# Row-block buffers in the dense stage of a fused layer's training step, attention weights loaded among its row blocks, and the first left rows and masks kept on chip

## The chip, the cores and the metric

The kernel runs on one core of one Trainium2 chip, as a single launch. The metric is the device time of that launch in microseconds (us); less is better. Before the change, three runs took 2913.0, 2915.46 and 2922.69 us, so the median is 2915.46 us.

## What is computed

The reference is one layer, forward and backward. `xn` is the layer norm of `x` (2048 rows of 512). Two branches start from it, and the output is `x + attention(xn) + dense(xn)`; then come the gradients of ten inputs.

```
def _A_ref(x, mem0, Wq, Wk, Wv, Wo, seg_len):      # 64 segments of 32 rows, 8 memory rows, 32 heads of 128
    mem = mem0
    for s in range(n_seg):
        h = concatenate([mem, x of segment s])
        q, k, v = h Wq, h Wk, h Wv
        p = softmax(where(mask, q k^T * scale, -1e9))
        o = (p v) Wo
        mem = o[:, :M, :]                           # the next segment starts from these rows
        outs.append(o[:, M:, :])
def _B_ref(x, w1, b1, w2, b2):                      # 512 -> 1792 -> 512
    r = relu(x w1 + b1)
    return (r * r) w2 + b2
```

All arrays are bfloat16. The attention branch is a recurrence over 64 segments; the dense branch is not.

## The kernel before, in words

The launch has five stages, one behind the other: the dense branch with its backward pass (this is the stage that changes), the "left rows" (attention projections that can be made ahead of the recurrence), the forward recurrence, the backward recurrence with left blocks, and the weight gradients. The order inside the recurrences is written out by hand (`F_ORDER`, `B_ORDER`, under `manual_schedule`). In the dense stage and the left rows a scheduler places the instructions of each engine, the DMA issues of the SP queue among them; the order in the source is only its starting point.

**Dense stage (L176 to L329).** 2048 rows are worked in `NRB` = 4 row blocks of `RB` = 512 rows. Block `rb` does the following.

- `norm(rb)` (L193 to L218) normalises the rows on DVE (`bn_stats` L198, `xn` L206) with one `sqrt` on ACT (L202), stores them (`S_XN`, L209), turns them with 16 PE transposes (`ps_tr`) into `HT` (L215) and stores `HT` in four pieces (`S_HX`, L218). It is called for block `rb + 1` inside block `rb`, behind the second matrix product below.
- `ps_h` (L271): 14 groups of 4 matmuls; ACT makes `rT` = relu (L273), DVE makes `aT` = rT * rT (L274).
- `ps_ga` (L278): 14 groups of 4 matmuls on the turned output gradient `gT`; DVE makes `gh1T` (L280).
- Then, for each of four row chunks `rc` of 128 rows: `ps_B` (L302, 14 matmuls), evacuated by two DVE additions (L305, L307; the second adds `x`, read again from DRAM as `xb`, L297) and stored (`S_B`, L308); `ps_gxb` (L311, 14 matmuls), copied (L314) and stored (`S_GXNB`, L315); 28 transposes of `aT` and `gh1T` (`ps_trf`), copied into `Nt` (L323) and stored (`S_AN` and `S_GH1N`, L324). `Nt` has two buffers, so a chunk's copy waits until the store of the chunk before it has landed. All PSUM tiles of the stage turn through eight buffers (`pst`).

`HT` and `gT` hold all 2048 rows for the whole stage; `rT` and `gh1T` are two tiles. In the last block GpSimd copies the first 8 rows of each segment out of them into `xl` and `gl`, and those go to DRAM (`S_XL`, L259, and `S_GLT`, L264).

**Weights.** `weight_load(1)` fetches `Wk` (4 MB) in one DMA on SP (L182, placed by the scheduler into block 0). `Wq` and `Wv` (4 MB each) are fetched in the last block, after `ps_ga`, on GpSimd's queue, into the room that the tiles of pool `p1c` leave.

**Left rows (L334 to L366).** `XL0`, `XL1` (from `S_XL`) and `Wo` (4 MB) are loaded on SP (L356 to L358). 30 groups of 4 matmuls (`ps_L`, L349) follow in the order of `ALL_LEFT`: 8 groups with `Wk` and `XL0`, 6 with `Wk` and `XL1`, 8 with `Wq`, 8 with `Wv`. ACT and DVE copy each group into half of a `dNL` tile (L364; six buffers), and each full tile is stored into `S_NL` (L353, 15 stores).

**Start of the forward recurrence.** GpSimd builds the masks `maskA` and `maskl1` (L676 to L689), DVE copies `maskl1` into `maskL` (L697). `memN0` is loaded and turned by four small transposes (`ps_m0`), `X0` is loaded from `S_HX` (L961), and its memory rows are written by DVE (L962). The first projections (L391) read `X0`; their results go into `f_N` (L373, L376), whose room was that of some `dNL` tiles, and are then turned (`ps_tr`, L164).

Of the kernel before, what the change touches and what calls it, by code (L numbers as in the profile page):

```python
# [26 lines left out]
def kernel(  # L27
# [92 lines left out]
    S_XL = dram.tile([P, DC, S // SEG * M], BF16, name="S_XL")  # L120
# [33 lines left out]
    rstd_t = const.tile([P, TC], F32, name="rstd_t")  # L154

# [11 lines left out]
    ht_cm = sb("ht", 1)  # L167
    htp = ht_cm.__enter__()
    HT = htp.tile([P, DC, S], BF16, name="HT")

# [5 lines left out]

    RCB = RB // P
    wk_cm = sb("wk", 1, "right")
    Wqkv = [None, wk_cm.__enter__().tile([P, DC, HD], BF16, name="Wk"), None]

    def weight_load(t, q=dma):
        q(Wqkv[t][:], (A_Wq, A_Wk, A_Wv)[t].rearrange("(c p) h e -> p c (h e)", p=P))  # L182
    with sb("p1b", 2) as p1b, sb("p1", 1) as p1:
        p1c_cm = sb("p1c", 1)
        p1c = p1c_cm.__enter__()
        xq = {}

        def x_load(rb):
            xq[rb] = p1b.tile([P, RCB, D], BF16, name="xq", tag="xq")
            dma(xq[rb][:], xflat[rb * RB:(rb + 1) * RB, :].rearrange("(c p) d -> p c d", p=P))  # L190

        def norm(rb):

            x = xq[rb]
            bs_ = p1b.tile([P, RCB, 6], F32, name="bs_", tag="bs_")
            mv = p1b.tile([P, RCB, 2], F32, name="mv", tag="mv")
            for c in range(RCB):
                nc.vector.bn_stats(bs_[:, c, :], x[:, c, :])  # L198
                nc.vector.bn_aggr(mv[:, c, :], bs_[:, c, :])
            veps = p1b.tile([P, RCB], F32, name="veps", tag="veps")  # L200
            nc.vector.tensor_scalar(out=veps[:], in0=mv[:, :, 1], scalar1=EPS, scalar2=None, op0=ALU.add)
            nc.scalar.sqrt(veps[:], veps[:])  # L202
            nc.vector.reciprocal(rstd_t[:, rb * RCB:(rb + 1) * RCB], veps[:])
            xn = p1b.tile([P, RCB, D], BF16, name="xn", tag="xn")
            for c in range(RCB):
                nc.vector.tensor_scalar(out=xn[:, c, :], in0=x[:, c, :], scalar1=mv[:, c, 0:1],  # L206
                                        scalar2=rstd_t[:, rb * RCB + c:rb * RCB + c + 1], op0=ALU.subtract,
                                        op1=ALU.mult)
            dma(S_XN[rb * RB:(rb + 1) * RB, :].rearrange("(c p) d -> p c d", p=P), xn[:])  # L209
            for d0 in range(0, DC, 2):  # L210
# [4 lines left out]
                nc.any.tensor_copy(HT[:, d0:d0 + 2, rb * RB:(rb + 1) * RB], ps[:])  # L215
            for c in range(RCB):
                b0 = rb * RB + c * P
                dma(S_HX[b0 // P], HT[:, :, b0:b0 + P])  # L218

# [5 lines left out]
        gT = p1c.tile([P, DC, S], BF16, name="gT")  # L225

        def g_load(rb):
            nc.sync.dma_start_transpose(gT[:, :, rb * RB:(rb + 1) * RB], gflat[rb * RB:(rb + 1) * RB, :])
            dma(S_GT[:, :, rb * RB:(rb + 1) * RB], gT[:, :, rb * RB:(rb + 1) * RB])
# [11 lines left out]
        for f0 in range(0, FC, 2):  # L241
            nc.sync.dma_start_transpose(W1T[:, f0:f0 + 2, :], B_w1[:, f0 * P:(f0 + 2) * P])
        b2bc = p1.tile([P, D], BF16, name="b2bc")
# [6 lines left out]
        for rb in range(NRB):  # L250
            r0 = rb * RB
            if rb == NRB - 1:
                xl = p1c.tile([P, DC, NB * NL], BF16, name="xl", tag="xl")
                for dc in range(DC):
                    for q in range(NB // SPB):
                        nc.gpsimd.tensor_copy(
                            xl[:, dc, q * P:(q + 1) * P].rearrange("p (j t b) -> p b j t", t=M, b=SPB),
                            HT[:, dc].rearrange("p (q b j r) -> p q b j r", b=SPB, j=SPB, r=SEG)[:, q, :, :, 0:M])
                dma(S_XL[:], xl[:])  # L259
                gl = p1c.tile([P, DC, NB * NL], BF16, name="gl", tag="xl")  # L260
                for dc in range(DC):
                    nc.gpsimd.tensor_copy(gl[:, dc].rearrange("p (s t) -> p s t", t=M),
                                          gT[:, dc].rearrange("p (s r) -> p s r", r=SEG)[:, :, 0:M])
                dma(S_GLT[:], gl[:])  # L264
            rT = p1c.tile([P, FC, RB], BF16, name="rT")
            aT = p1.tile([P, FC, RB], BF16, name="aT")
            gh1T = p1.tile([P, FC, RB], BF16, name="gh1T")
            for fc in range(FC):
                ps = pst([P, RB], F32, name="ps_h1")
                for dc in range(DC):  # L270
                    nc.tensor.matmul(ps[:], lhsT=W1[:, dc, fc * P:(fc + 1) * P], rhs=HT[:, dc, r0:r0 + RB],  # L271
                                     start=(dc == 0), stop=(dc == DC - 1))
                nc.scalar.activation(rT[:, fc, :], ps[:], ACT.Relu, bias=b1T[:, fc:fc + 1], scale=1.0)  # L273
                nc.vector.tensor_tensor(out=aT[:, fc, :], in0=rT[:, fc, :], in1=rT[:, fc, :], op=ALU.mult)  # L274
            for fc in range(FC):
                ps2 = pst([P, RB], F32, name="ps_ga")
                for dc in range(DC):
                    nc.tensor.matmul(ps2[:], lhsT=W2T[:, dc, fc * P:(fc + 1) * P], rhs=gT[:, dc, r0:r0 + RB],  # L278
                                     start=(dc == 0), stop=(dc == DC - 1))
# [4 lines left out]
            if rb == NRB - 2:  # L284
                weight_load(1)
# [3 lines left out]
            else:  # L289
# [3 lines left out]
                for t, n in ((0, "Wq"), (2, "Wv")):  # L293
                    Wqkv[t] = wqp.tile([P, DC, HD], BF16, name=n)
                    weight_load(t, pdma)
            xb = p1b.tile([P, RCB, D], BF16, name="xb", tag="xb", bufs=1)
            dma(xb[:], xflat[r0:r0 + RB, :].rearrange("(c p) d -> p c d", p=P))  # L297
            for rc in range(RCB):
# [17 lines left out]
                for srcT, dstD in ((aT, S_AN), (gh1T, S_GH1N)):  # L316
# [7 lines left out]
                    dma(dstD[:, :, rr0 // P, :].rearrange("n p f -> p n f"), Nt[:].rearrange("p (n f) -> p n f", f=2 * P))  # L324
        gb1s = p1.tile([P, FC], F32, name="gb1s")
# [4 lines left out]
    ht_cm.__exit__(None, None, None)  # L330

# [8 lines left out]
    ALL_LEFT = (ALL_LEFT[:n_k] + ALL_LEFT[3 * n_k:3 * n_k + PER] + ALL_LEFT[n_k:3 * n_k] + ALL_LEFT[3 * n_k + PER:])  # L340
# [13 lines left out]
    with sb("fl", 2) as fl:  # L354
        XL0 = fl.tile([P, DC, P], BF16, name="XL0", bufs=1)
        dma(XL0[:], S_XL[:, :, 0:P])  # L356
        dma(XL1[:], S_XL[:, :, P:])
# [313 lines left out]
    with sb("fw", 1) as fw, psum("fr", 4) as fr, psum("fpp", 1) as fpp, \  # L671
            ExitStack() as fstack:

        KM = 4
        maskA = fw.tile([P, KM, KW], BF16, name="maskA")
        nc.gpsimd.memset(maskA[:], 0.0)  # L676
        maskL = fw.tile([P, KM, KW], BF16, name="maskL")
        maskl1 = fw.tile([P, 2, SPB, M], F32, name="maskl1")
        nc.gpsimd.memset(maskl1[:], 0.0)

        def keep(ap, pattern, base, mul):
            nc.gpsimd.affine_select(ap, ap, pattern=pattern, compare_op=ALU.is_ge, fill=-1e9, base=base,
                                    channel_multiplier=mul)

        for g in range(HG):
            sl = slice(32 * g, 32 * g + 32)

            keep(maskA[sl, :, M:SEG], [[0, KM], [-1, XS]], -M, 1)
            nc.gpsimd.memset(maskA[32 * g:32 * g + M, :, :], 0.0)  # L689

            keep(maskl1[sl, 0], [[-M, SPB], [0, M]], 0, 1)
            keep(maskl1[sl, 0], [[M, SPB], [0, M]], M - 1, -1)
            keep(maskl1[sl, 1], [[-M, SPB], [-1, M]], 0, 1)
            keep(maskl1[sl, 1], [[-M, SPB], [0, M]], 0, 1)
            keep(maskl1[sl, 1], [[M, SPB], [0, M]], M - 1, -1)
        for k in range(KM):
            nc.vector.tensor_copy(maskL[:, k, :], maskl1[:].rearrange("p a j m -> p (a j m)"))  # L697
# [11 lines left out]
        memN = fo.tile([M, D], BF16, name="memN0")  # L709
        dma(memN[:], mem0flat)  # L710
        psm0 = tr("ps_m0")
        for dc in range(DC):
            transpose_to(psm0[:, dc * M:(dc + 1) * M], memN[:, dc * P:(dc + 1) * P])
# [5 lines left out]
        def block(b):  # L719

            if b not in blk:
# [8 lines left out]
                def make(n):  # L730
                    pool, shape, dt = shapes[n]
                    return pool.tile(shape, dt, name=n, tag=n)
# [227 lines left out]
        X0 = block(0)["X"]  # L960
        dma(X0[:], S_HX[0])  # L961
        nc.vector.tensor_copy(X0[:, :, 0:M], psm0[:, 0:DC * M].rearrange("p (c m) -> p c m", c=DC))  # L962
# [19 lines left out]
    xl_cm.__exit__(None, None, None)  # L982
    assert not TURNS_O
# [3 lines left out]
    with sb("la", 2) as la, sb("ls", 2) as ls, sb("lo", 1) as lo_, sb("wg", 2) as wg, psum("lpp", 1) as lpp, psum("lr", 4) as lr:  # L987
# [122 lines left out]
        def keep(b, i, ps):  # L1110
# [4 lines left out]
            if "b2" in ps and i == 0:  # L1115
                ps["b2s"] = wg.tile([1, D], BF16, name="gb2b", bufs=1)
# [557 lines left out]
```

## Time and profile before

| | |
|---|---|
| median of the runs | 2915.46 us |
| time of the profiled execution | 2925.15 us |
| its span | 2923.3 us |
| mean granted TensorE clock | 0.973 |
| PE busy | 2721.1 us (93%) |
| DVE, ACT, POOL busy | 1297.6, 1030.6, 655.3 us |
| dense stage on PE | 9.71 to 262.4 us |
| left rows on PE | 268.18 to 296.4 us |
| first projection of the forward recurrence | 300.99 us |

The profile is one execution. The span runs from its first to its last instruction; 1.85 us of the execution's time lie outside it. A row of the timeline of an engine gives the start, the length, the line, the operation and tiles, the count, and in brackets the idle time ahead of it with what ended that. "Granted clock" is the share of TensorE's full clock in a stretch. On the SP queue the rows are DMA issues, not transfers; where an issue row is long, the queue was held.

### The profile page before, as it was taken

The page shows a single profiled execution, that of the slowest core. Times are in us where ns is not written, and L with a number is a line of the kernel's source. Part 1 is how long each engine was busy: PE and PEld are TensorE (multiplying, and loading weights), DVE is VectorE, ACT ScalarE, POOL GpSimd, SP SyncE. Part 2 cuts the span into 40 slices and gives each one's busy share as a digit, 9 for nine tenths or more (in the row PEclk, how much of TensorE's full clock was granted, in tenths as well). Part 3 has the DMA queues.
Part 4 walks back from the last instruction along what each step waited for, and adds up shares of the span by engine and source line. Part 5 has one row for each costly group of instructions (what it writes and reads, how often), then busy time and mean ns, then how long its engine had stood idle before and what let it go on. Part 6 is the DMA issues. An engine that isn't in the chain of part 4 may idle for free.

```text
span 2923.3 us, 116288 instructions
## 1 busy us (share of the span) xinstructions
PE 2721.1 (93%) x51700; PEld 1476.2 (50%) x51700; DVE 1297.6 (44%) x3790; ACT 1030.6 (35%) x2362; POOL 655.3 (22%) x1262
## 2 busy tenths in 40 slices
PE   7997899999999888889899999998999899999999
PEld 3453455555555555547445545554555444444444
DVE  5452466666666565444445544554455401100000
ACT  2332354444544444433333433433343301111111
POOL 0000100000000001122434343343333324332221
PEclk9998899999999999899899999999999999999999
DMA  9639367677776676999577777777777799999993
GB/s 249 214 101 292 94 166 191 178 193 184 181 196 171 166 170 167 230 260 259 145 181 176 175 197 202 177 183 201 189 172 184 215 280 226 222 211 234 205 206 79
DMA packets 796536, 564.17 MB, mean 193 GB/s; under 512 B 584593, under 2 KB 687138, under 8 KB 792706
## 3 DMA queue, kind: packets, MB, share of 16 engines
q1 hardware_dynamic: 753922, 424.58, 63.3%
q0 software_dynamic: 42112, 132.16, 14.4%
q8 instruction: 405, 6.64, 1.0%
q14 instruction: 97, 0.79, 0.1%
HBM read 191.51 MB, written 234.37 MB: 146 GB/s over the span
## 4 chain that ended last, share of the span: by engine, by line
PE 77%; DMA 11%; DVE 5%; SPq 3%; issue 3%; ACT 1%; POOL 0%; ACTq 0%; DVEq 0%; POOLq 0%
PE ps_gw L1635 17%; PE ps_proj L391 15%; PE ps_gR L459 11%; PE ps_R L459 5%; PE ps_L L349 3%; PE b_pp L589 3%; PE ps_tr L164 3%; PE ps_RL L1247 3%; DMA b_kLs<-S_NL 3%; PE ps_w L1102 2%; PE ps_sc L436 2%; PE f_pp L589 2%; PE b_T L494 1%; PE f_T L494 1%; PE ps_w L1097 1%
## 5 line engine op out<-in xcount | busy, mean ns | idle before, releaser
L1635 PE MATMUL ps_gw<-gn,HNc 128*128 128x512 bf16 x1920 | 416.8, 379 | 0.0
L1635 PEld LDWEIGHTS <-HNc 128*128 128x128 bf16 x1920 | 187.8, 98 | 223.6
L373 ACT CAST f_N<-ps_proj 128x512 bf16<-128x512 f32 x320 | 183.8, 580 | 202.5 <-PE ps_proj L391 200.9
L1568 ACT CAST wt<-ps_gw 128x512 bf16<-128x512 f32 x128 | 74.1, 587 | 450.6 <-PE ps_gw L1635 402.2
L391 PEld LDWEIGHTS <-X 128*32 128x32 bf16 x6144 | 154.3, 96 | 149.8 <-DVE X L503 21.4
L1551 DVE TENSOR_TENSOR gx<-ps_rows,gb 128x512 f32<-128x512 f32 x16 | 11.1, 692 | 426.6 <-PE ps_rows L1549 426.6
L891 POOL COPY kM<-f_kT 128x256 bf16<-128x256 bf16 x64 | 25.6, 400 | 739.9 <-DVE f_kT L376 565.9
L1635 PE MATMUL ps_gw<-GOc,gn 128*128 128x512 bf16 x640 | 141.6, 384 | 10.9 <-ACT wt L1568 9.4
L459 PE MATMUL ps_gR<-Wv,gv 128*32 128x512 bf16 x2048 | 145.9, 407 | 1.2 <-issue 1.2
L391 PE MATMUL ps_proj<-Wq,X 128*32 128x512 bf16 x2048 | 136.1, 382 | 7.2 <-DVE X L962 4.5
L459 PE MATMUL ps_gR<-Wk,gk 128*32 128x512 bf16 (+1 forms) x2048 | 141.1, 390 | 1.4 <-ACT gk L373 0.7
L373 ACT CAST gk<-b_pp 128x256 bf16<-128x256 f32 x192 | 70.7, 379 | 179.7 <-PE b_pp L589 116.0
L459 PE MATMUL ps_R<-Wo,OT 128*32 128x256 bf16 x4096 | 132.9, 286 | 1.1 <-DVE OT L376 1.1
L391 PE MATMUL ps_proj<-Wk,X 128*32 128x512 bf16 x2048 | 133.1, 384 | 0.7
L373 ACT CAST gON<-ps_proj 128x512 bf16<-128x512 f32 x128 | 74.9, 585 | 156.9 <-PE ps_proj L391 156.9
L391 PE MATMUL ps_proj<-Wv,X 128*32 128x512 bf16 x2048 | 129.9, 378 | 0.0
L391 PE MATMUL ps_proj<-Wo,GT 128*32 128x512 bf16 x2048 | 124.2, 384 | 4.2 <-DVE GT L1292 3.5
L1569 POOL DMA_DIRECT2D out_dram<-wt x120 | 64.8, 542 | 258.3 <-ACT wt L1568 243.5
L459 PE MATMUL ps_gR<-Wq,gq 128*32 128x512 bf16 (+1 forms) x2048 | 118.5, 343 | 0.9 <-issue 0.9
L1328 POOL COPY PD<-b_P 32x320 bf16<-32x320 bf16 x256 | 114.7, 448 | 8.0
L459 PEld LDWEIGHTS <-OT 128*32 128x32 bf16 x4096 | 108.1, 101 | 9.3 <-DVE OT L376 1.3
L1323 POOL DMA_DIRECT2D b_P<-S_A x63 | 33.8, 537 | 336.9 <-issue 103.5
(281 smaller groups left out, 5352.6 us busy)
## 6 DMA issues: line engine op xcount, KB each, us to landing
S_A<-f_N SPq DMA_DIRECT2D x64, 512.0 KB
out_dram<-wt POOLq DMA_DIRECT2D x134, 128.0 KB, 5.1
S_A<-f_N SPq DMA_DIRECT2D x64, 256.0 KB
S_GB<-gv SPq DMA_DIRECT2D x32, 512.0 KB
S_GB<-gq SPq DMA_DIRECT2D x32, 512.0 KB
S_GB<-gk SPq DMA_DIRECT2D x32, 512.0 KB
b_kN<-S_A POOLq DMA_DIRECT2D x63, 256.0 KB, 4.5
b_qN<-S_A POOLq DMA_DIRECT2D x63, 256.0 KB, 3.9
```

The source lines that it names most:

```text
L164: nc.tensor.transpose(ps_ap, in_ap, ident[base:base + k, base:base + k])
L349: nc.tensor.matmul(ps[:], lhsT=x(dc), rhs=Wqkv[t][:, dc, c0:c0 + 512], start=(dc == 0), stop=(dc == DC - 1))
L373: nc.scalar.copy(out, in_)
L391: nc.tensor.matmul(o, lhsT=hT[:, dc, :], rhs=x, start=(dc == 0), stop=(dc == DC - 1), tile_position=(0, 32 * g))
L436: nc.tensor.matmul(sc3[32 * g:32 * g + 32, k, c:c + n], lhsT=qT[:, 4 * h + k, g, :], rhs=kT[:, 4 * h + k, g, :], start=(mask is None), sto ...
L459: nc.tensor.matmul(R[32 * g:32 * g + 32, 0:(cs.stop - cs.start) * P].rearrange("p (a b) -> p a b", b=P), lhsT=XT(k, g), rhs=x[:, cs, :], s ...
L589: nc.tensor.matmul(o, lhsT=N_[32 * g:32 * g + m, kk * P:(kk + 1) * P], rhs=X(kk)[32 * g:32 * g + m], start=(i == 0), stop=(i == len(jobs) ...
L1247: nc.tensor.matmul(ps["R", i][32 * g:32 * g + 32, :].rearrange("p (a b) -> p a b", b=P), lhsT=B_[n][:, k, g, :], rhs=W(g * KH + k), start= ...
L1328: nc.gpsimd.tensor_copy(PD[32 * g:32 * g + 32, g], C["P"][32 * g:32 * g + 32, :, 0:L])
L1568: nc.scalar.copy(wt[:], ps[:])
L1569: eng(dst, wt[:])
L1635: nc.tensor.matmul(ps[:], lhsT=l(rc), rhs=r(rc), start=(n == 0), stop=(n == RC_ALL - 1))
```

## The change

- `HT` and `gT` become tiles of one row block (512 rows, one buffer each). `rT` and `gh1T` become one tile: relu is written into it, and the gradient replaces it in place.
- `x` has three buffers instead of two, and the addition of `x` (L307, now L345) reads it there; `xb` and its four loads go.
- `first_rows(rb)` copies each block's first rows on GpSimd as soon as the block is there. Those of the first 16 segments stay on chip (`XLa`); the rest go to DRAM once. The whole first 128 rows stay too (`Xa`), with the memory rows written into them in block 1 (`memN0`, four transposes, one DVE copy).
- `Wv` gets room of its own beside `Wk` from the start. The weights are fetched in 1 MB pieces on SP: one piece behind each row chunk, `Wk` in block 1, `Wv` in block 2, `Wq` in block 3, as the source has it. Nothing is fetched on GpSimd's queue in this stage.
- In the last block GpSimd copies `XLa` and `Xa` to `XL0` and `X0` and finishes the masks there; `maskA` is 40 columns wide instead of 64.
- The left rows go `Wk`/`XL0` (8 groups), `Wv`/`XL0` (8), `Wk`/`XL1` (6), `Wq`/`XL0` (8).
- `gb2b`, a small tile of a later stage, takes a turn in the buffers of `wt2`.

```diff
-    HT = htp.tile([P, DC, S], BF16, name="HT")
...
-    Wqkv = [None, wk_cm.__enter__().tile([P, DC, HD], BF16, name="Wk"), None]
-    def weight_load(t, q=dma):
-        q(Wqkv[t][:], (A_Wq, A_Wk, A_Wv)[t].rearrange("(c p) h e -> p c (h e)", p=P))
+    Wqkv = [None, wkp.tile([P, DC, HD], BF16, name="Wk"), wkp.tile([P, DC, HD], BF16, name="Wv")]
+    def weight_load(t, dc):
+        dma(Wqkv[t][:, dc], (A_Wq, A_Wk, A_Wv)[t].rearrange("(c p) h e -> c p (h e)", p=P)[dc])
...
-            xq[rb] = p1b.tile([P, RCB, D], BF16, name="xq", tag="xq")
+            xq[rb] = p1b.tile([P, RCB, D], BF16, name="xq", tag="xq", bufs=3)
...
+            HT = HTs[rb] = p1.tile([P, DC, RB], BF16, name="HT")
...
+        def first_rows(rb):
+            for dc in range(DC):
+                nc.gpsimd.tensor_copy(
+                    (xl[:, dc, (rb - 1) * P:rb * P] if rb else first["XLa"][:, dc]).rearrange("p (j t b) -> p b j t", t=M, b=SPB),
+                    HTs[rb][:, dc].rearrange("p (b j r) -> p b j r", b=SPB, j=SPB)[:, :, :, 0:M])
+                nc.gpsimd.tensor_copy(gl[:, dc, rb * P:(rb + 1) * P].rearrange("p (s t) -> p s t", t=M),
+                                      gTs[rb][:, dc].rearrange("p (s r) -> p s r", r=SEG)[:, :, 0:M])
+            if rb == 0:
+                nc.gpsimd.tensor_copy(first["Xa"][:, :, M:], HTs[0][:, :, M:P])
+            if rb == 1:
+                ps = pst([P, DC * M], BF16, name="ps_m0")
...
-            rT = p1c.tile([P, FC, RB], BF16, name="rT")
-            gh1T = p1.tile([P, FC, RB], BF16, name="gh1T")
+            rT = gh1T = p1.tile([P, FC, RB], BF16, name="gh1T")
...
-            if rb == NRB - 2:
-                weight_load(1)
...
-                for t, n in ((0, "Wq"), (2, "Wv")):
-                    Wqkv[t] = wqp.tile([P, DC, HD], BF16, name=n)
-                    weight_load(t, pdma)
-            xb = p1b.tile([P, RCB, D], BF16, name="xb", tag="xb", bufs=1)
-            dma(xb[:], xflat[r0:r0 + RB, :].rearrange("(c p) d -> p c d", p=P))
+                Wqkv[0] = wqp.tile([P, DC, HD], BF16, name="Wq")
+                XL0, X0 = (smp.tile([P, DC, P], BF16, name=n) for n in ("XL0", "X0"))
+                nc.gpsimd.tensor_copy(XL0[:], first["XLa"][:])
+                nc.gpsimd.tensor_copy(X0[:], first["Xa"][:])
+                maskA, maskL = masks(smp, p1)
+            xb = xq[rb]
...
+                if rb:
+                    weight_load((None, 1, 2, 0)[rb], rc)
...
-    ALL_LEFT = (ALL_LEFT[:n_k] + ALL_LEFT[3 * n_k:3 * n_k + PER] + ALL_LEFT[n_k:3 * n_k] + ALL_LEFT[3 * n_k + PER:])
+    ALL_LEFT = (ALL_LEFT[:n_k] + ALL_LEFT[2 * n_k:3 * n_k] + ALL_LEFT[3 * n_k:3 * n_k + PER] + ALL_LEFT[n_k:2 * n_k]
+                + ALL_LEFT[3 * n_k + PER:])
...
-        dma(XL0[:], S_XL[:, :, 0:P])
-        dma(XL1[:], S_XL[:, :, P:])
+        dma(XL1[:], S_XL[:])
...
-        X0 = block(0)["X"]
-        dma(X0[:], S_HX[0])
-        nc.vector.tensor_copy(X0[:, :, 0:M], psm0[:, 0:DC * M].rearrange("p (c m) -> p c m", c=DC))
```

More of the change, by code (lines that the diff above doesn't have):

```diff
@@ L119 @@
     S_HX = dram.tile([S // P, P, DC, P], BF16, name="S_HX")
-    S_XL = dram.tile([P, DC, S // SEG * M], BF16, name="S_XL")
+    S_XL = dram.tile([P, DC, S // SEG * M - P], BF16, name="S_XL")
     S_GM = dram.tile([NB, P, D], BF16, name="S_GM")
@@ L175, in pst, with masks, keep @@
         return psp.tile(shape, dt, name=name, tag="ps")
+    def masks(pool, temp):
+        maskA = pool.tile([P, KM, L], BF16, name="maskA")
+        maskL = pool.tile([P, KM, KW], BF16, name="maskL")
+        maskl1 = temp.tile([P, 2, SPB, M], F32, name="maskl1")
+        nc.gpsimd.memset(maskA[:], 0.0)
+        nc.gpsimd.memset(maskl1[:], 0.0)
+        def keep(ap, pattern, base, mul):
+            nc.gpsimd.affine_select(ap, ap, pattern=pattern, compare_op=ALU.is_ge, fill=-1e9, base=base,
+                                    channel_multiplier=mul)
+        for g in range(HG):
+            sl = slice(32 * g, 32 * g + 32)
+            keep(maskA[sl, :, M:SEG], [[0, KM], [-1, XS]], -M, 1)
+            nc.gpsimd.memset(maskA[32 * g:32 * g + M, :, :], 0.0)
+            keep(maskl1[sl, 0], [[-M, SPB], [0, M]], 0, 1)
+            keep(maskl1[sl, 0], [[M, SPB], [0, M]], M - 1, -1)
+            keep(maskl1[sl, 1], [[-M, SPB], [-1, M]], 0, 1)
+            keep(maskl1[sl, 1], [[-M, SPB], [0, M]], 0, 1)
+            keep(maskl1[sl, 1], [[M, SPB], [0, M]], M - 1, -1)
+        for k in range(KM):
+            nc.gpsimd.tensor_copy(maskL[:, k, :], maskl1[:].rearrange("p a j m -> p (a j m)"))
+        return maskA, maskL
     RCB = RB // P
     wk_cm = sb("wk", 1, "right")
-    Wqkv = [None, wk_cm.__enter__().tile([P, DC, HD], BF16, name="Wk"), None]
-    def weight_load(t, q=dma):
-        q(Wqkv[t][:], (A_Wq, A_Wk, A_Wv)[t].rearrange("(c p) h e -> p c (h e)", p=P))
+    wkp = wk_cm.__enter__()
+    Wqkv = [None, wkp.tile([P, DC, HD], BF16, name="Wk"), wkp.tile([P, DC, HD], BF16, name="Wv")]
+    def weight_load(t, dc):
+        dma(Wqkv[t][:, dc], (A_Wq, A_Wk, A_Wv)[t].rearrange("(c p) h e -> c p (h e)", p=P)[dc])
     with sb("p1b", 2) as p1b, sb("p1", 1) as p1:
@@ L185 @@
         p1c = p1c_cm.__enter__()
-        xq = {}
+        xq, HTs, gTs = {}, {}, {}
+        first = {n: p1.tile([P, DC, P], BF16, name=n) for n in ("XLa", "Xa")}
+        xl = p1c.tile([P, DC, (NRB - 1) * P], BF16, name="xl")
+        gl = p1c.tile([P, DC, NB * NL], BF16, name="gl")
         def x_load(rb):
-            xq[rb] = p1b.tile([P, RCB, D], BF16, name="xq", tag="xq")
+            xq[rb] = p1b.tile([P, RCB, D], BF16, name="xq", tag="xq", bufs=3)
             dma(xq[rb][:], xflat[rb * RB:(rb + 1) * RB, :].rearrange("(c p) d -> p c d", p=P))
@@ L214, in norm @@
                         transpose_to(ps[:, dc - d0, c * P:(c + 1) * P], xn[:, c, dc * P:(dc + 1) * P])
-                nc.any.tensor_copy(HT[:, d0:d0 + 2, rb * RB:(rb + 1) * RB], ps[:])
+                nc.any.tensor_copy(HT[:, d0:d0 + 2, :], ps[:])
             for c in range(RCB):
-                b0 = rb * RB + c * P
-                dma(S_HX[b0 // P], HT[:, :, b0:b0 + P])
+                if rb or c:
+                    dma(S_HX[rb * RCB + c], HT[:, :, c * P:(c + 1) * P])
+        def first_rows(rb):
[9 more added lines that the diff above has]
+                ps = pst([P, DC * M], BF16, name="ps_m0")
+                for dc in range(DC):
+                    transpose_to(ps[:, dc * M:(dc + 1) * M], memN[:, dc * P:(dc + 1) * P])
+                nc.vector.tensor_copy(first["Xa"][:, :, 0:M], ps[:].rearrange("p (c m) -> p c m", c=DC))
+            if rb == NRB - 1:
+                dma(S_XL[:], xl[:])
+                dma(S_GLT[:], gl[:])
         W1 = p1c.tile([P, DC, F], BF16, name="W1")
@@ L242 @@
             nc.sync.dma_start_transpose(W1T[:, f0:f0 + 2, :], B_w1[:, f0 * P:(f0 + 2) * P])
+        memN = p1.tile([M, D], BF16, name="memN0")
+        dma(memN[:], mem0flat)
         b2bc = p1.tile([P, D], BF16, name="b2bc")
@@ L251 @@
             r0 = rb * RB
[L252 to L264, printed above, removed]
-            rT = p1c.tile([P, FC, RB], BF16, name="rT")
+            HT, gT = HTs[rb], gTs[rb]
+            first_rows(rb)
             aT = p1.tile([P, FC, RB], BF16, name="aT")
-            gh1T = p1.tile([P, FC, RB], BF16, name="gh1T")
+            rT = gh1T = p1.tile([P, FC, RB], BF16, name="gh1T")
             for fc in range(FC):
@@ L277 @@
                 for dc in range(DC):
-                    nc.tensor.matmul(ps2[:], lhsT=W2T[:, dc, fc * P:(fc + 1) * P], rhs=gT[:, dc, r0:r0 + RB],
+                    nc.tensor.matmul(ps2[:], lhsT=W2T[:, dc, fc * P:(fc + 1) * P], rhs=gT[:, dc, :],
                                      start=(dc == 0), stop=(dc == DC - 1))
@@ L670 @@
         "L.E0 L.E3 L.E5 L.oa1 L.ob1 L.pm0 L.pm1 L.ra k0Te k1Te oa1 pm0 pm1 q0Te q0ev")
-    with sb("fw", 1) as fw, psum("fr", 4) as fr, psum("fpp", 1) as fpp, \
+    with psum("fr", 4) as fr, psum("fpp", 1) as fpp, \
             ExitStack() as fstack:
[L674 to L697, printed above, removed]
         def big(name):
@@ L730, in make @@
                 def make(n):
+                    if n == "X" and b == 0:
+                        return X0
                     pool, shape, dt = shapes[n]
```

23 lines of the change are left out of this document (9 added, 14 removed).

## The prediction

> **What bounds the kernel now.** I read the engine table first: PE is busy 93% of the span, and the chain that ended last is mostly PE's own work, so whatever PE does not wait for costs nothing.
>
> ```profile
> span 2923.3 us, 116288 instructions
> PE 2721.1 (93%) x51700; PEld 1476.2 (50%) x51700; DVE 1297.6 (44%) x3790; ACT 1030.6 (35%) x2362; POOL 655.3 (22%) x1262
> PE 77%; DMA 11%; DVE 5%; SPq 3%; issue 3%; ACT 1%; POOL 0%; ACTq 0%; DVEq 0%; POOLq 0%
> ```
>
> The change ends before the forward recurrence begins, so next I read PE's timeline from 0 to 310 us, for brackets (idle time ahead of a row, and who ended it).
>
> ```profile
> 77.05 10.52 PE L271 MATMUL ps_h<-HT,W 128*128 128x512 bf16 x48
> 91.49 3.56 PE L271 MATMUL ps_h<-HT,W 128*128 128x512 bf16 x8 [3.91 <-DVE Nt L323]
> ...
> 252.42 1.65 PE L164 MATMUL ps_trf<-ident,gh1T 128*128 128x128 bf16 x14 [12.23 <-ACT Nt L323]
> 253.86 3.95 PE L302 MATMUL ps_B<-W,aT 128*128 128x512 bf16 x14
> ...
> 268.18 14.37 PE L349 MATMUL ps_L<-Wk,XL 128*128 128x512 bf16 x56 [5.78 <-DMA XL<-S_XL]
> 282.38 7.07 PE L349 MATMUL ps_L<-Wq,XL 128*128 128x512 bf16 x32
> ...
> 300.99 1.90 PE L391 MATMUL ps_proj<-Wq,X 128*32 128x512 bf16 x16 [4.45 <-DVE X L962]
> ```
>
> Four gaps touch the change: 3.91, 12.23, 5.78 and 4.45, in all 26.4 us. (A fifth, 5.60 us at 38.8, waits for the second block's `xn`; its loads keep their places on SP, so it stays.) After each gap the same matmuls are slow: 8 took 3.56 us where 8 of the 48 before take 1.75; 56 left-row matmuls took 14.37, where 32 take 7.07, so 56 would take 12.37. The windows show why: the granted clock falls to half.
>
> ```profile
> 266.00:268.00 2.00, 0.00 (x0) 0.00 (x0) 0.00 (x0) 0.00 (x0) 0.00 (x0) 0.50 0.78 173
> 268.00:270.00 2.00, 1.82 (x5) 0.73 (x6) 0.00 (x0) 0.00 (x0) 0.00 (x0) 0.50 0.98 320
> 274.00:276.00 2.00, 2.00 (x11) 0.93 (x10) 1.01 (x2) 0.58 (x1) 0.00 (x0) 1.00 1.09 348
> 302.00:304.00 2.00, 2.00 (x28) 0.68 (x20) 0.00 (x0) 0.00 (x0) 1.77 (x8) 0.50 0.20 46
> ```
>
> (The last three numbers of a row are clock, DMA share and GB/s.) Last, the SP and ACT timelines, for who is late behind the gaps:
>
> ```profile
> 72.62 1.19 SPq L182 DMA_DIRECT2D Wk<-in_A_Wk_dram  x1
> 222.65 12.09 SPq L308 DMA_DIRECT2D S_B<-Bt  x1
> 266.52 0.62 SPq L358 DMA_DIRECT2D Wo<-in_A_Wo_dram  x1
> 283.17 1.24 ACT L364 CAST dNL<-ps_L 128x512 bf16<-128x512 f32 x2 [2.59 <-DMA S_NL<-dNL]
> ```
>
> The first gap is `Nt` waiting for a store of the chunk before (ACT's copy starts at 90.82), and that store stood behind the 4 MB of `Wk`. The second is the same while `Wq` and `Wv` load from GpSimd's queue; SP was held 12.09 us at one store.
>
> **The change, part by part.**
>
> *Gap 12.23 (last block).* In the changed program's order `Wv` stands on SP at the end of block 0, for the time of block 1's products; such a time needs few transfers (0 GB/s from 150.0 to 157.5 us, in block 2's). Only `Wq` is left for the last block, four pieces of 1 MB: SP issues two when `ps_ga` ends (their room is that of `W1`, `W2T` and `gT`), the others behind the first and the second chunk's `S_B`. The third chunk's `Nt` copy is the one at risk: ahead of the store that it waits for stand `Wq` and two chunks' stores of 1.28 MB, 6.6 MB, 19 us at 350 GB/s (row 274); from `ps_ga`'s end (218.0) to that copy (239.2) there are 21 us. They fit. Saved: 12.23, and the slow rows behind it, 1.65 - 0.95 and 3.95 - 3.19: **13.7 us**. If a piece holds a store after all, up to 4 come back.
>
> *Gap 3.91 (block 1).* Ahead of the late store now stand three 1 MB pieces instead of 4 MB (3 us less), and `xb`, the last `x` load and the next `gT` are gone from that place (0.5 MB each, some 1.5, 1.5 and 3.3 us by their SP rows); the landing moves from 90.7 to about 80. But ACT's two `Nt` copies now stand ahead of all relus of the next block (before, eight relus went first), so PE stalls when the PSUM buffer of the first `Nt` is wanted, at 77.3 + 3 x 0.864 = 79.9. The `sqrt` of the last block also moves among those relus, behind an `x` load that lands at about 83; it ends near 88 and is wanted at 88.5. Both about even; I leave 1 us. Saved: 3.91 + 1.81 - 1.0 = **4.7 us** (5.7 down to 0, if the landing is 4 us later than I think).
>
> *Gaps 5.78 and 4.45, the left rows and the start.* `XL0` and `X0` are now GpSimd copies made some 20 us before they are wanted (GpSimd's mask work was 7.8 us, 296.4 to 304.0, the copies are two more of about 1 us). PE begins the left rows at once. What is late next? `Wo`. Before, SP issued it at 266.52, 1.7 us ahead of the first left-row matmul, and the first `dNL` store, which stood behind it, landed at 283.17, 16 us after `Wo`'s issue. In the changed program `XL1` and `Wo` lie on the `Nt`, `S_GXNB` and `S_B` buffers of the last chunk and wait for those stores: issue ends about 5.4 us after PE starts. The first store then lands at 21.4. The seventh `dNL` tile needs the first one's buffer; with eight PSUM buffers PE can go on until its 21st group, at 20 x 0.864 = 17.3, and resumes 0.7 after the landing: a new stall of **4.8 us**, and 2.0 more for the slow clock behind it (14.37 - 12.37, behind the gap nearest in length). Left rows: 120 x 0.216 = 25.9, + 4.8 + 2.0 = 32.7 us. Then `f_N`: its room is that of the last two `dNL` tiles now (before, of the last but one), so its first copy waits for the last `S_NL` store: 0.7 copy, 0.5 issue, 2.3 landing, 0.7 own copy, 4.2 us; the projections run meanwhile (3.6 at full clock). So the first turns of `f_N` come 36.9 us after the dense stage's last transposes. Before it was 307.38 - 262.40 = 45.0. Saved: **8.1 us**. Ends: no stall at all gives 25.9 + 3.6 and 15.5 saved; a `Wo` later by 5 more gives 3.
>
> On the clock, the Trainium skill ("TensorE: Matmul & The Clock Gate", Part 1: The HAM clock gate) says an idle window of about 3.4 us drops the clock to half, and 3.4 us of work brings it back. The trace agrees on the half (0.50) and on gaps of 3.9 us and more, and its slow stretch is nearer 4.7 us; by the page the stall would cost 1.7 more instead of 2.0, and the sum would be 26.8.
>
> *Costed at nothing.* In place `gh1T`: same instructions on ACT and DVE (L273, L274, L280), and the next block's relus come after the last transposes of `gh1T` in PE's order anyway. Single `HT`: its copies wait for the `S_HX` stores issued at 41 to 45, and stand at 47.0 (ACT) and 50.4 (DVE) already; 1 us on ACT at worst, under product rows that need no `HT`. Single `gT`: the load of the next one waits on SP until `ps_ga` ends; behind it stand stores of later tiles alone, and its data are wanted 40 us on. `first_rows`: 8 GpSimd copies of 0.33 us, GpSimd idle. `maskA` of 40 columns: same 0.23 us matmul. The four small transposes (0.25 us) move, and are on PE in both. From the second step of the recurrence on, the order on every engine is the same.
>
> Sum: 13.7 + 4.7 + 8.1 = **26.5 us**, 2925.15 to 2898.7 for the profiled execution. That lies 9.7 above the median of 2915.46, and nothing in this stage explains the offset, so I take the difference from the median: **2889 us**.
>
> **Rivals.**
>
> *A: the left rows do not stall.* If the first `dNL` store lands by 17 us after the start, 4.8 + 2.0 us are saved too: 2882, to 2880. For it: its margin was 4 us before. Against it: `Wo` is issued 7 us later relative to PE. 0.17.
>
> *B: the stores stay late.* The weight pieces in block 0 hold `Nt` as `Wk` did (nothing saved there, 4.7), or those of the last block cost 4, or `Wo` costs 5 more: 2894 to 2904. For it: DMA share is 1.0 from 25 to 100 us. 0.18.
>
> *C: slower.* SP is one list. Each of the twelve pieces stands ahead of stores whose landing frees `Nt`. Price: 12 x 3 = 36 us if every piece holds PE for its whole length; above 26.5 the change loses: 2889 + 36 = 2925. It decides where PE's lead over the stores is under 3 us. The trace speaks against it: PE ran 10.5 us (the 48-matmul row) past the chunk before it stopped for 4 MB. The Trainium skill ("DMA: Bandwidth & Descriptors", Queues, rings and completion order) has each DMA engine take a ring's descriptors in order, which is this rival's mechanism; the store behind `Wk` agrees. 0.04.
>
> *D: the change doesn't do what it says.* If the room of `Wq` came free only with the last chunk, its 4 MB would load under the left rows, ahead of `Wo` (12 us more), and most of the gain is given back: 2901 to 2915. The built order shows the wait on `ps_ga` alone. 0.06.
>
> **How the numbers follow.** Forecast (2885 to 2893) 0.55, A 0.17, B 0.18, C 0.04, D 0.06. The range of 8 in 10 takes in A, the forecast and most of B: 2880 to 2902. A measurement of this kernel tells about 0.3%, 8.7 us, from no change: faster means below 2906.7. Forecast, A, B and a third of D: 0.92; within 0.3%, the rest of D and the edge of C: 0.05; slower, the rest of C: 0.03.
>
> **What would show it.** PE's timeline: no bracket over 1.5 us in `ps_h` of block 1 and in `ps_trf` of the last block; `ps_L` beginning within 0.5 us of the last `ps_trf`, and one bracket of 3 to 6 us inside `ps_L`, ended by a `dNL` copy that waits for `S_NL`; the first `ps_proj` directly behind `ps_L`; turns of `f_N` about 37 us after the last `ps_trf`. Wrong if a bracket over 2 us stands in block 1 or 2, or if the recurrence, from 320 us on, differs in length by over 3 us.

## The result, and the profile after

The changed kernel takes **2903.9 us** (median of six runs, 2896.93 to 2908.18); beside them the kernel before took 2914.23 (six runs, 2910.18 to 2922.69). The ratio is **0.9959, 95% interval 0.9939 to 0.9979**: faster by about 12 us (6 to 18), where 26.5 were forecast; the range on record was 2880 to 2902. The profiled execution took 2896.93 us, with a granted clock of 0.978.

First the page of the changed kernel: span, engine table and chain.

```profile
span 2894.9 us, 116348 instructions
PE 2713.6 (94%) x51700; PEld 1472.0 (51%) x51700; DVE 1298.9 (45%) x3786; ACT 1029.3 (36%) x2362; POOL 658.1 (23%) x1279
PE 79%; DMA 9%; DVE 5%; SPq 3%; issue 3%; ACT 2%; POOL 0%; ACTq 0%; DVEq 0%; POOLq 0%
```

The span is 28.4 us shorter, PE's busy time only 7.5: what went is waiting. The 28.4 is not the gain: this profile is of the shortest of its six runs, and that of before took 10.9 us more than the median beside it. PE's timeline shows where the waiting went (start, length, line, tiles, count; in brackets the idle time ahead and who ended it).

```profile
77.81 12.26 PE L308 MATMUL ps_h<-HT,W 128*128 128x512 bf16 x56
...
242.63 0.94 PE L165 MATMUL ps_trf<-ident,gh1T 128*128 128x128 bf16 x14
243.41 3.62 PE L388 MATMUL ps_L<-Wk,XL 128*128 128x512 bf16 x16
250.98 5.12 PE L388 MATMUL ps_L<-Wk,XL 128*128 128x512 bf16 x16 [3.96 <-ACT Nt L361]
...
263.20 3.62 PE L388 MATMUL ps_L<-Wk,XL 128*128 128x512 bf16 x16
273.25 3.57 PE L388 MATMUL ps_L<-Wk,XL 128*128 128x512 bf16 x8 [6.44 <-ACT dNL L401]
276.62 7.74 PE L388 MATMUL ps_L<-Wq,XL 128*128 128x512 bf16 x32
...
288.74 1.24 PE L165 MATMUL ps_tr<-ident,f_N 128*128 128x128 bf16 x16 [0.81 <-DVE f_N L413]
```

The same two places in PE's timeline of the kernel before:

```profile
261.45 0.94 PE L164 MATMUL ps_trf<-ident,gh1T 128*128 128x128 bf16 x14
...
307.31 1.16 PE L164 MATMUL ps_tr<-ident,f_N 128*128 128x128 bf16 x16
```

The brackets of 3.91 (block 1), 12.23 (last block), 5.78 and 4.45 are gone. The last `ps_trf` ends at 243.6 (before, 262.4), and the left rows follow at once. But the left rows now hold two brackets, 3.96 and 6.44, and the first turns of `f_N` come 45.2 us behind the last `ps_trf`; before it was 44.9. So of 18.8 us won in the dense stage, 18.6 are left at the first turns (288.74 against 307.31), and nothing was won between.

Who holds the left rows? SP's queue (issues) and ACT's timeline of the changed kernel:

```profile
229.70 1.98 SPq L369 DMA_DIRECT2D out_dram<-gb1b  x1
232.86 1.50 SPq L346 DMA_DIRECT2D S_B<-Bt  x1
...
243.45 3.84 SPq L346 DMA_DIRECT2D S_B<-Bt  x1
...
256.01 0.38 SPq L395 DMA_DIRECT2D Wo<-in_A_Wo_dram  x1
```

```profile
249.92 1.01 ACT L361 COPY Nt<-ps_trf 128x1024 bf16<-128x1024 bf16 x1 [6.89 <-DMA S_AN<-Nt]
...
272.62 2.46 ACT L401 CAST dNL<-ps_L 128x512 bf16<-128x512 f32 x4 [12.95 <-DMA S_NL<-dNL]
```

`Wo` is issued 12.6 us after the first left-row matmul; I had said 5.4. It waits for the last chunk's stores, and those hardly moved, as the windows show (the busy time of the five engines, then clock, DMA share, GB/s).

```profile
228.00:232.00 4.00, 4.00 (x25) 1.94 (x23) 1.37 (x3) 1.25 (x2) 0.00 (x0) 1.00 1.01 353
232.00:236.00 4.00, 4.00 (x41) 2.63 (x39) 1.36 (x3) 1.50 (x2) 0.00 (x0) 1.00 1.22 154
236.00:240.00 4.00, 4.00 (x20) 1.86 (x19) 0.00 (x0) 0.00 (x0) 0.00 (x0) 1.00 1.42 26
240.00:244.00 4.00, 4.00 (x41) 2.64 (x40) 1.85 (x3) 1.50 (x2) 0.00 (x0) 1.00 0.95 40
...
272.00:274.00 2.00, 0.75 (x2) 0.26 (x2) 1.36 (x3) 1.31 (x3) 0.00 (x0) 0.50 0.99 382
```

From 236 to 244 the DMA engines are as busy as at 228, and move a tenth of the bytes. The packets are tiny: of the 3182 from 232 to 244 us, 1854 have under 512 bytes. The one transfer of that kind that SP issues there is `out_dram<-gb1b` (L369, the bias gradient): 3.5 KB, written to DRAM as 1792 separate values of 2 bytes. The kernel before has the same store, and its windows show the same drop inside the 12.23 us gap. Its SP queue and windows:

```profile
219.37 0.38 SPq L329 DMA_DIRECT2D out_dram<-gb1b  x1
```

```profile
236.00:240.00 4.00, 4.00 (x30) 2.22 (x29) 0.00 (x0) 0.00 (x0) 0.00 (x0) 1.00 1.01 416
...
244.00:248.00 4.00, 0.00 (x0) 0.00 (x0) 0.00 (x0) 0.00 (x0) 0.00 (x0) 0.65 1.03 82
```

### The profile page after: what moved, and what is told of

Same layout as the page of the kernel before. It is cut to its first block, busy times and chain, and to the rows that moved or that the text cites. A ratio compares the mean times of both kernels' runs of the same rounds, so it can differ in the third digit from the quotient of the medians.

```text
span 2894.9 us, 116348 instructions
## 1 busy us (share of the span) xinstructions
PE 2713.6 (94%) x51700; PEld 1472.0 (51%) x51700; DVE 1298.9 (45%) x3786; ACT 1029.3 (36%) x2362; POOL 658.1 (23%) x1279
## 4 chain that ended last, share of the span: by engine, by line
PE 79%; DMA 9%; DVE 5%; SPq 3%; issue 3%; ACT 2%; POOL 0%; ACTq 0%; DVEq 0%; POOLq 0%
PE ps_gw L1643 16%; PE ps_proj L428 15%; PE ps_gR L496 11%; PE ps_R L496 5%; PE b_pp L626 3%; PE ps_tr L165 3%; PE ps_L L388 3%; PE ps_RL L1255 3%; DMA b_kLs<-S_NL 2%; PE ps_w L1110 2%; PE ps_sc L473 2%; PE f_pp L626 2%; PE ps_B L340 2%; PE f_T L531 2%; PE b_T L531 2%
## 5 line engine op out<-in xcount | busy, mean ns | idle before, releaser
L901 POOL COPY kM<-f_kT 128x256 bf16<-128x256 bf16 x64 | 25.6, 401 | 736.7 <-DVE f_kT L413 562.7
```

## The experiments

Two theories at the start. **S**: the 2-byte store holds the stores behind it, and with them `Wo` and the left rows. **W**: the 1 MB pieces of `Wq` in the last block do. Ratios are to the kernel before, run beside it on the same chip; its own median was 2914 to 2931 us from one comparison to the next, so times of different comparisons aren't set against each other.

**The bias gradient as rows** (in the changed kernel, and alone in the kernel before): turned on PE, stored as 14 rows of 256 bytes.

```diff
-        dma(out_8.rearrange("(c p) -> p c", p=P), gb1b[:])
+        ps = pst([FC, P], BF16, name="ps_b1")
+        transpose_to(ps[:], gb1b[:])
+        gb1r = p1.tile([FC, P], BF16, name="gb1r")
+        nc.vector.tensor_copy(gb1r[:], ps[:])
+        dma(out_8.rearrange("(c p) -> c p", p=P), gb1r[:])
```

> The changed kernel, but the bias gradient (out_8, 1792 values) is turned on PE and stored as 14 rows of 256 bytes instead of 1792 values of 2 bytes. Theory S (the 2-byte store holds the DMA engines from about 232 to 242 us: share above 1.0 at 16 to 66 GB/s): in the last block no Nt copy waits over 1.5 us, the left rows begin without the 3.96 us bracket, Wo is issued about 5 us after they begin instead of 12.6, one bracket of about 5 us stays inside them, and the first turns of f_N come about 37 us after the last ps_trf instead of 45: 8 us less than the changed kernel, about 2895.5 us. Theory W (the four Wq pieces hold the stores): the waits at 236 to 250 us stay, 2904 us, no difference over 2 us.

PE's timeline of the changed kernel with bias rows, then `Wo` on its SP queue, then its windows:

```profile
244.49 7.08 PE L392 MATMUL ps_L<-Wk,XL 128*128 128x512 bf16 x31
...
266.57 3.57 PE L392 MATMUL ps_L<-Wk,XL 128*128 128x512 bf16 x8 [4.64 <-ACT dNL L405]
...
281.74 1.25 PE L165 MATMUL ps_tr<-ident,f_N 128*128 128x128 bf16 x16 [1.13 <-DVE f_N L417]
```

```profile
249.69 0.38 SPq L399 DMA_DIRECT2D Wo<-in_A_Wo_dram  x1
```

```profile
236.00:240.00 4.00, 3.95 (x30) 2.19 (x29) 1.26 (x3) 1.69 (x2) 0.00 (x0) 1.00 0.72 226
240.00:244.00 4.00, 4.00 (x38) 2.49 (x36) 1.53 (x3) 1.12 (x2) 0.00 (x0) 1.00 0.32 106
```

The stretch of 26 to 40 GB/s and the 3.96 bracket are gone, with `Wq`'s pieces where they were: theory S holds, theory W falls. `Wo` is issued 5.2 us after the first left-row matmul (forecast: 5.4). What stays is the bracket that I had forecast, 4.64 against 4.8, and the first turns come 37.3 us behind the last `ps_trf` (forecast: 36.9). Ratio 0.9922 (0.9892 to 0.9953).

> The kernel before, with the bias gradient stored as 14 rows, nothing else changed. Theory S: part of the 12.23 us gap at 240 us belongs to the 2-byte store too, since GB/s fell to 82 there at a share of 1.03: the gap shrinks to under 6 us and the kernel gains 6 to 9 us, about 2907. Theory W: the gap is the 8 MB of Wq and Wv alone and stays at 11 us or more: 2913 to 2915.

In the kernel before, the same edit halves the gap of the last block (12.23 before):

```profile
243.22 1.65 PE L164 MATMUL ps_trf<-ident,gh1T 128*128 128x128 bf16 x14 [6.32 <-ACT Nt L323]
```

Under 6 us was expected, so this is a near miss. The first turns come 10.0 us earlier in the trace. The timed ratio, 0.9986 (0.9961 to 1.001), can't tell that from nothing, and a gain of 6 to 9 us was expected.

The row store also stands later on SP than the 2-byte store did (245.93 instead of 229.70 in the changed kernel, 255.18 instead of 219.37 in the kernel before). So these two runs change the store's form and its place together; the run with the 2-byte store issued late, below, tells them apart in part.

**Fifteen `dNL` buffers** (`bufs=6` becomes `bufs=15` at the tile of L398), with and without bias rows.

> As e1_bias_rows, and 15 dNL buffers instead of 6, so that no copy of a left row waits for a store. If the bracket inside ps_L is the wait for dNL buffers behind Wo: no bracket there, full clock, left rows in 26 us; the S_NL stores then all stand behind Wo and end about 30 us after the left rows begin, where f_N and the first f_vLs wait for some of them: 3 to 7 us less than e1, about 2890. If that wait only moves to f_N or f_vLs in full, the same as e1.

> The changed kernel with 15 dNL buffers alone, the 2-byte store as it was. The 3.96 us bracket ahead of the 17th left-row matmul stays (it is Nt), the 6.44 us bracket and its slow rows go; f_N waits for the late stores instead: 2 to 6 us less than the changed kernel, 2898 to 2902. If neither of the two is on the path: 2904.

With both edits no bracket is left in the left rows; they take 26 us. PE's timeline behind them:

```profile
274.16 1.25 PE L165 MATMUL ps_tr<-ident,f_N 128*128 128x128 bf16 x16
...
276.89 0.28 PE L477 MATMUL ps_sc<-f_kT,f_qT 128*32 128x40 bf16 x16 [1.42 <-POOL f_kT L904]
```

Ratios 0.9898 (0.9865 to 0.9931) with both, 0.9922 (0.9894 to 0.9951) with the buffers alone, where the `Nt` bracket stays (3.00) and the other goes. The buffers alone so won some 11 us over the changed kernel's 0.9959, where 2 to 6 were expected; the intervals overlap.

**Sixteen `wt` buffers.** In the weight-gradient stage far behind the change, one stall of `ps_gw` took 9.4 us before and 6.9 after, and 6 to 17 in four variants. Does the change give part of its gain back there?

```diff
+             sb("p5w", 16) as p5w, \
...
-            wt = p5.tile([P, 512], BF16, name="wt5", tag="wt5", bufs=6)
+            wt = p5w.tile([P, 512], BF16, name="wt5", tag="wt5")
```

> The kernel before, with 16 buffers instead of 6 for the tile wt of the weight-gradient stage; nothing else changes. In that stage one stall of ps_gw behind ACT wt took 9.4 us in the kernel before, 6.9 in the changed one, and 6 to 17 us in four variants of them. Theory N (noise: the stall is a store that lands late, by an amount that varies from execution to execution in every variant): the stall is gone here, the time is 5 to 10 us below the kernel before (ratio about 0.9975), and the runs spread less. Theory G (the changed kernels pay more at that stall, and so give part of their gain back): here little is won, under 4 us, and the changed kernel wins over 8 by the same edit.

> The changed kernel with the same 16 buffers for wt. In the traces the first turns of f_N come 18.6 us earlier than in the kernel before, and the timed gain was 12 (6 to 18). Theory N: the stall is gone in both, and the difference to the kernel before with 16 buffers is the 18.6 us of the forward stage, give or take 4. Theory G: the difference is larger, 22 to 28 us, since what was given back at the stall is kept. A third case, a difference of 12 or less, would put the give-back somewhere else, in the recurrence.

Both expected that the stall would go. It only moved, from ACT's `wt` to the loads. The waits of PE, first of the kernel before with 16 buffers, then of the changed one (us in all, times, longest):

```profile
PE ps_gw L1636 <- DMA gn<-S_GL: 7.4, 2, 5.5
PE ps_gw L1636 <- DMA GOc<-S_GM: 6.0, 1, 6.0
```

```profile
PE ps_gw L1644 <- DMA gn<-S_GL: 7.1, 4, 4.6
PE ps_gw L1644 <- DMA GOc<-S_GM: 4.6, 1, 4.6
PE ps_gw L1644 <- DMA gn<-S_OL: 2.7, 1, 2.7
```

Ratios 1.0003 (0.998 to 1.0025) and 0.996 (0.9932 to 0.9988). With 16 buffers the wait is for loads of that stage, not for a buffer, and its sum is about the same in both kernels. The medians differ by 12.8 us, which is neither theory N (14.6 to 22.6) nor theory G (22 to 28), but close to the third case; the intervals are too wide to settle it. The stalls over 15 us did stand in variants of the changed kernel alone, but the changed kernel itself had 6.9, so that they belong to the change isn't shown.

> The changed kernel with three edits: the bias gradient out_8 turned on PE and stored as 14 rows of 256 bytes, 15 instead of 6 dNL buffers, and 16 instead of 6 wt buffers. The first two put the first turns of f_N at 274 us (14.6 earlier than in the changed kernel); under theory N the third takes the 7 to 16 us stall out of the weight-gradient stage. Sum: about 20 us below the changed kernel, ratio to the kernel before about 0.988. Rival: the weight-gradient stage is held by the stores as a whole, its stall moves to a later tile, and the time is that of the kernel with the first two edits (0.990).

0.9884 (0.9852 to 0.9916), the lowest ratio of all, first turns at 274.20. It can't be told from the two edits without the `wt` buffers (0.9898), so the buffers earn nothing that shows; the rival expected that.

**The weights back on GpSimd's queue.**

> The changed kernel with Wq and Wv loaded whole (4 MB each) from GpSimd's queue in the last block, as in the kernel before; Wk stays in 1 MB pieces on SP, and everything else of the change stays, the 2-byte store of the bias gradient too. Theory P (the 12.23 us gap of the last block was mostly these 8 MB beside the Nt stores, so that the placement of the weights removed it): a bracket of 6 to 13 us ended by ACT Nt is back in ps_trf of the last block, the first turns of f_N come 6 to 14 us later than in the changed kernel (295 to 303 us), and the time is 2910 to 2918 on the scale on which the changed kernel is 2904. Rival (the gap was the 2-byte store alone, which the kernel before also had there): the bracket stays under 4 us and the time equals the changed kernel's within 3 us.

This run (e7) went wrong as an experiment. `Wv` has its own room in the changed kernel, so its load waited for nothing and started at once. GpSimd's timeline, then PE's:

```profile
1.31 0.90 POOL L330 DMA_DIRECT2D Wv<-in_A_Wv_dram  x1 [0.37 <-issue]
```

```profile
20.80 15.07 PE L308 MATMUL ps_h<-HT,W 128*128 128x512 bf16 x55 [7.22 <-DMA W<-in_B_w_dram]
47.00 10.47 PE L315 MATMUL ps_ga<-gT,W2T 128*128 128x512 bf16 x39 [9.39 <-ACT gh1T L310]
...
257.90 1.65 PE L165 MATMUL ps_trf<-ident,gh1T 128*128 128x128 bf16 x14 [5.99 <-ACT Nt L363]
```

The two brackets cost 16.6 us in the first block, ahead of the stage it was to test (ratio 1.0003). The next two put `Wv` into the room that the last `ps_ga` frees, as before:

```diff
-                Wqkv[0] = wqp.tile([P, DC, HD], BF16, name="Wq")
+                for t, n in ((0, "Wq"), (2, "Wv")):
+                    Wqkv[t] = wqp.tile([P, DC, HD], BF16, name=n)
+                    pdma(Wqkv[t][:], (A_Wq, A_Wk, A_Wv)[t].rearrange("(c p) h e -> p c (h e)", p=P))
...
-                if rb:
-                    weight_load((None, 1, 2, 0)[rb], rc)
+                if rb == 1:
+                    weight_load(1, rc)
```

> The changed kernel with Wq and Wv both loaded whole from GpSimd's queue in the last block, into the room that the last ps_ga leaves, as in the kernel before (the run e7 let Wv start at 1.3 us, which cost its first block 17 us). The 2-byte store stays. Theory P (both crowd the last block: weights about 6 us, store about 6): a bracket of 9 to 13 us ended by ACT Nt is back in ps_trf; the stores then are done when the left rows begin, so that the 3.96 bracket there goes, and f_N is first turned at 295 to 301 us; time ratio to the kernel before 0.997 to 0.999. Rival (the store alone made the gap): bracket about 6, f_N at 289 to 292, ratio 0.996 or less.

> The same, with the bias gradient stored as 14 rows of 256 bytes, so that the 8 MB on GpSimd's queue are alone with the last block's stores. Theory P: a bracket of about 6 us (6.3 in the kernel before with these rows) in ps_trf, f_N at 286 to 290 us, where the same kernel with Wq in pieces on SP had no bracket and 281.7; ratio about 0.994. Rival (the store alone): no bracket over 2 us, f_N at 282.

PE's timelines, first with the 2-byte store, then with bias rows:

```profile
248.84 1.65 PE L165 MATMUL ps_trf<-ident,gh1T 128*128 128x128 bf16 x14 [12.45 <-ACT Nt L363]
...
282.35 3.56 PE L390 MATMUL ps_L<-Wk,XL 128*128 128x512 bf16 x8 [6.35 <-ACT dNL L403]
```

```profile
242.88 1.65 PE L165 MATMUL ps_trf<-ident,gh1T 128*128 128x128 bf16 x14 [6.40 <-ACT Nt L363]
```

12.45 stands where 12.23 stood, and 6.40 where the kernel before with bias rows had 6.32. So half of the old gap was the 8 MB of weights and half the 2-byte store; the placement of the weights removed the first half, and the second came back as a bracket in the left rows. One expectation was missed: with bias rows the first turns came at 291.06, not at 286 to 290. Ratios 0.9978 (0.9949 to 1.0007) and 0.9943 (0.992 to 0.9965), against 0.9955 to 0.9959 and 0.9922 with the weights in pieces on SP; the intervals overlap, so the price of the placement rests on the traces.

**The 2-byte store, late.** It is written into a `dNL` buffer behind the left rows' tiles, and issued behind most of their stores.

```diff
+        gb1b = fl.tile([P, GW], BF16, name="gb1b", tag="dNL", bufs=15)
+        nc.vector.tensor_copy(gb1b[:, 0:FC], gb1s[:])
+        dma(out_8.rearrange("(c p) -> p c", p=P), gb1b[:, 0:FC])
```

> The changed kernel with 15 dNL buffers, and the bias gradient stored as it was, in 1792 values of 2 bytes, but issued behind most of the left rows' stores (it is written into a dNL buffer, and so waits for the first of them). Tells the store's place from its form. If the place decided: no bracket in ps_L, f_N turned at about 274 us, and the time is that of the kernel with bias rows and 15 buffers, ratio 0.990. If the form costs wherever it stands: the same 274 us, but the loads of the left K and V rows behind it on SP are held by about 10 us, a new bracket of 5 to 10 us stands ahead of the first scores or their product with the left rows, and the ratio is 0.992 to 0.994.

PE's timeline, SP's queue and the windows of this kernel:

```profile
275.21 1.25 PE L165 MATMUL ps_tr<-ident,f_N 128*128 128x128 bf16 x16 [0.41 <-DVE f_N L413]
292.55 0.32 PE L473 MATMUL ps_sc<-f_kT,f_qT 128*32 128x40 bf16 x16 [16.02 <-POOL f_kT L900]
```

```profile
272.62 0.58 SPq L403 DMA_DIRECT2D out_dram<-gb1b  x1
288.56 1.28 SPq L635 DMA_TRANSPOSE kL<-S_NL  x1
```

```profile
276.00:278.00 2.00, 0.52 (x6) 0.37 (x6) 0.73 (x3) 1.49 (x3) 0.00 (x0) 1.00 0.42 0
...
284.00:286.00 2.00, 0.00 (x0) 0.00 (x0) 0.00 (x0) 0.00 (x0) 0.00 (x0) 0.50 0.00 0
```

The left rows run free, and the load of `kL`, next on SP, is issued 15.9 us after the store: a bracket of 16.02 where 5 to 10 were expected. SP's waits name the store:

```profile
SPq L635 <- DMA out_dram<-gb1b: 15.3, 1, 15.3
```

So the 2-byte form costs in this place too; whether rows of 256 bytes would be free in the early place was not tried. Ratio 0.9929 (0.9901 to 0.9957), inside what was expected for this case, but it overlaps with that of the rows (0.9898), and the trace is of the longest of the eleven runs (2933.84 us, median 2912.03). So the 16.02 may be more than usual.

**The changed kernel again.**

> The changed kernel as it is, once more beside the kernel before. Dense-stage traces of two pairs (before and its 16-wt variant, first f_N turns at 307.4 and 305.5 us; changed and its 16-wt variant, 288.7 and 288.6) give 17.8 us. If the stages behind give nothing back, the timed ratio is 0.994 (0.992 to 0.996); if a third of the gain is given back behind the dense stage, it is 0.996 (0.995 to 0.998) as in the first comparison.

0.9955 (0.9934 to 0.9976), by the medians 2915.06 against 2931.12: the first result, again. It lies between the two cases that were to be told apart (0.994 and 0.996), and its interval takes in both. In this trace the first bracket of the left rows is 5.25 instead of 3.96, and the first turns come at 292.55.

All kernels together: the first turns of `f_N` (before: 307.31), how much earlier that is, and the timed gain, (1 - ratio) x 2914. Each timed gain is uncertain by 6 to 10 us either way. The kernel with the late 2-byte store is left out, because its 16 us wait comes behind the first turns.

| kernel | first turns, us | earlier by | timed gain, us |
|---|---|---|---|
| changed | 288.74 | 18.6 | 12 |
| changed, again | 292.55 | 14.8 | 13 |
| changed, 16 `wt` | 288.58 | 18.7 | 12 |
| changed, 15 `dNL` | 280.30 | 27.0 | 23 |
| changed, bias rows | 281.74 | 25.6 | 23 |
| changed, bias rows, 15 `dNL` | 274.16 | 33.2 | 30 |
| the same, 16 `wt` | 274.20 | 33.1 | 34 |
| changed, `Wq` and `Wv` on GpSimd | 297.59 | 9.7 | 6 |
| the same, bias rows | 291.06 | 16.3 | 17 |
| before, bias rows | 297.36 | 10.0 | 4 |
| before, 16 `wt` | 305.48 | 1.8 | -1 |
| changed, `Wv` at the start | 307.26 | 0.1 | -1 |

On the mean of these rows the timed gain is 3 us less than what was won at the first turns; part of that is that the one profile of the kernel before has its turns 1.8 us later than that of its 16-`wt` variant, whose code is the same up to there.

## Why the prediction came out too fast

- **Gaps 12.23 and 3.91: right for PE in the dense stage.** Foretold 13.7 + 4.7 = 18.4 us; the dense stage ends 18.8 us earlier. Of these 5.0 were won before the last block's `ps_B` (217.99 to 212.98) and 13.8 behind it. Block 1 has no bracket (ACT's two `Nt` copies there start at 78.5 and 79.7, against a landing "at about 80"). "They fit" was right for the `Wq` pieces alone: with bias rows no `Nt` copy of the last chunks waits, but in the changed kernel ACT's copies waited 5.58 and 6.89 us, and PE paid for that only in the left rows.
- **Gaps 5.78 and 4.45, the left rows and the start: wrong, and this is the step that failed.** Both brackets went, as foretold, but the term of 8.1 us measured -0.3 (44.9 before, 45.2 after). The sum said that `Wo`'s "issue ends about 5.4 us after PE starts", from the pace of the last chunk's stores; it was 12.6, because those stores stood behind the 2-byte store, which was not in the sum at all. Hence the stall of 6.44 instead of 4.8, and the 3.96 that nobody had foretold. With that store gone the same step gives 37.3 us for 36.9, and the sum would have held: 25.6 us at the first turns for 26.5 foretold.
- **What I could have read.** The store stands in the profile of before, on SP at 219.37, and 82 GB/s at a DMA share of 1.03 stands inside the 12.23 gap. I put that whole gap down to the weights; half of it was the store. When 8 MB went away, its other cause did not.
- **Rivals.** B has the right place and size ("`Wo` costs 5 more", 2894 to 2904), for a reason that it doesn't name: it was 7 more. A (no stall in the left rows) is what 15 buffers and bias rows make. C and D did not happen: no piece held PE, and the weights stand where the built order had them.
- **The rest, 18.6 in the trace against 12 timed, isn't settled.** The changed kernel's traces give 14.8 to 18.7 at the first turns, and the interval reaches to 18. Behind that point one execution says little: from the first turns to the first `ps_w` the same changed kernel took 905.7 us in one trace and 912.6 in the other, from there to the first `ps_gw` 1123.9 and 1132.6. My condition, a recurrence within 3 us, can't be read from single traces. From the first turns to the end of the span, three traces of kernels without the change take 2611.5 to 2616.0 us, and ten with it 2606.2 to 2626.3 (the late store left out). A give-back of a few us behind the dense stage is neither shown nor excluded.
- **The slow clock.** The "4.7 us" of the prediction fits none of its four gaps: in windows of 0.25 us the clock is full again 3.5, 3.0, 4.3 and 5.6 us after PE resumes behind the gaps of 3.91, 12.23, 5.78 and 4.45. The 2.0 us that the sum used come from the third.

The Trainium skill ("DMA: Bandwidth & Descriptors", Rules for kernel authors) says that a last dimension that isn't contiguous becomes one descriptor per element and should be rearranged. The trace agrees: from 225 to 262 us the changed kernel has 2053 packets under 512 bytes, with bias rows 291, and 1762 fewer is about the 1792 values (some records can be missing). In this case the store was worth 6 us of the old gap, and 7 us at the first turns of the changed kernel.

## What to carry to other kernels

Look for windows in which the DMA share is high and the GB/s low: a store of a few KB in 2-byte pieces can hold megabytes behind it. Before you count a gap as won, list everything in its queue: a gap with two causes doesn't go with one of them, it moves to the next wait. Turning a small vector on PE, so that it is stored in rows, cost one matmul and one copy, and won 7.0 us at the first turns of `f_N` (10.0 in the kernel before), with the store issued later as well.

## What the runs showed of the hardware

- While a store of 1792 values of 2 bytes was under way, the DMA engines were busy for some 12 us (232 to 244) at 26 to 154 GB/s, where 353 flowed just before; as 14 rows of 256 bytes, issued later, it left no mark in PE's timeline.
- Issued behind the left rows' stores, the same store came ahead of a load that SP issued 15.9 us later, and SP's waits put 15.3 us down to the store, although the trace has no bytes moving from about 279 to 288 us. What keeps the store unfinished in that time, and whether the load waits for the queue or for the store's buffer, the trace doesn't show.
- The granted clock was 0.50 in windows inside and behind the longer gaps: at 272 to 276 us in the changed kernel (around the 6.44 us gap), and from 282 us on in the 16 us wait.
